# Other places in a hand-planned order of work, the last chunk done for all u at once, and w_o loaded from ScalarE

## The chip, the cores and the metric

The kernel runs on one core of one Trainium2 chip. The metric is the device time of one execution in microseconds (us), the median of several runs. PE is TensorE, DVE is VectorE, ACT is ScalarE, POOL is GpSimd and SP is SyncE, which here issues most DMAs.

## The reference: what is computed

Two strided convolutions with gelu, a joint network, and all gradients. B = 2, T = 16000, D = V = 256, U = 8, three taps; everything in bf16.

```python
h = sum_i einsum("btc,cd->btd", xp[:, i:i+T], w1[i]);  h = gelu(h)[:, ::2]
f = sum_i einsum("btc,cd->btd", hp[:, i:i+T1], w2[i]);  f = gelu(f)[:, ::2]
fe = f @ w_f;  ge = g @ w_g
j = tanh(fe[:, :, None, :] + ge[:, None, :, :])
out = j @ w_o                      # (2, 4000, 8, 256)
# outputs: out and, for a given grad_out, the gradients of x, w1, w2, g, w_f, w_g, w_o
```

The joint part and its gradient are the bulk: 8000 places (b, t) times 8 values of u.

## The kernel before

**Tiling.** The 8000 places lie on one axis and are cut into 17 chunks: one of 256, fifteen of 512 and one of 64 places (`sizes`). A chunk of 512 is nb = 4 blocks of 128; the last is nb = 1, n_ = 64. One chunk holds the border between the two batches (`c.mid`, number CB).

**Stages.** Each chunk passes through three:
- `stage_a`: transposed x arrives in XC by a transposing DMA; conv1 at odd and even places, gelu and its derivative (`conv_gelu`, a Square, a Gelu and a Tanh on ACT and six operations on DVE), conv2 with a gelu, then FE = f w_f. HR is HT transposed by a DMA. From chunk NTR = 2 on, `fe_rows` puts FE row-wise in FER with PE transposes.
- `stage_j`: four pairs of u (`pair(up)`). Per pair: JT = tanh(FE + GE) on ACT, 4 activations; JR, the same row-wise (DVE add of FER and GEB, then ACT tanh; in chunks 0 and 1 PE transposes of JT instead); GWO, the gradient of w_o, as JR times GO in one PSUM bank that is kept over the whole kernel; GOT (GO transposed by a DMA) times WOT, multiplied on DVE with JSQ - 1 (JSQ = JT squared) into NGZ or ZS, whose free-axis sum goes to NGP, and added up in ZS, at last in GN; and out = JT w_o, evicted to OUT and stored. Line 315 is the helper `mm`, so all these matmuls have one line, and tiles tell them apart.
- `stage_de` of the chunk before: the gradient goes back through w_f, w2, w1 (GN, GH, GX) and the weight gradients are added up in ACC1, ACC2, ACCF from row-wise copies HR, GNR, GHR and XR.

**What sets the order of work.** The program records operations with `op(engine, cost, ...)`. Each has a place in a line of work, `F.now` or `at`, counted in places of the axis: chunk k begins at `t0 = c.q0`, and the stages of other chunks stand at fractions of it. `Flow.issue` then plays a model: at each step it emits the operation that can start first, on the engine whose start is earliest, and among those ready, the one of the smallest place. Costs come from `c_pe`, `c_act`, `c_dve`, and a DMA takes its size over a rate, plus `land`. What it emits is the static program order of each engine; nothing is decided at run time. Buffers (`F.cls`: 3 JT, 3 JR, 3 GOT, 4 GO, 3 OUT, 7 PSUM banks) are handed out in this order as well.

**The last chunk.** It runs through the same `pair(up)` with nb = 1 and n_ = 64: PE operands 64 wide, four GO loads, four GOT transposes and four stores of 64 KB each. Behind it `last_w1` does the w1 gradient of the last two chunks together, and the final stores follow.

**The start.** ACT issues the loads of w1 (three), w_f and w_g; SP those of x, w2 and the transposed XC of chunk 1; POOL those of g and w_o. The tiles of w1 and w2 are both called W in the trace. `warm` is an early Gelu on ACT that makes its table load happen early; `make_ge` needs WG, and `turn` transposes WO, WG, WF, W2 and W1 on PE.

Of the kernel before, what the change touches and what calls it, by code (L numbers as in the profile page):

```python
# [10 lines left out]
BF16 = mybir.dt.bfloat16  # L11
# [175 lines left out]


def c_pe(ns):
    return sum(max(n / 2.4 + 2.5, 25.0) for n in ns)  # L190


def c_act(n, psum=False, ptr=False):
# [17 lines left out]
def kernel(  # L211
# [28 lines left out]
    KT = 2  # L240
# [225 lines left out]
    def conv_gelu(g_, jobs, rd, h_buf, pre, ho, gname, gcls, gshape, gsave, news):  # L466
# [36 lines left out]
               r=[qk(mt), ps], w=[sk(mt)])  # L503
        k = GELU_A / 2
        N = KT * W
        late = F.now + CW * (0.8 if g_ == 1 else 0.25)
        go_ = 1 if gsave else 0
        full = lambda T_, o_=0: T_[:, o_:o_ + nb, :, :n_]
        op("ACT", c_act(N), lambda e: nc.scalar.activation(out=full(s, so), in_=full(s, so), func=ACT.Tanh, scale=k),  # L509
# [31 lines left out]
    def stage_a(g_, t0, dt):  # L541
        c = chunks[g_]
        S = st[g_]
        XC = S["XC"]
        nb, n_ = c.nb, c.np
        na = min(nb, 2)
        HT = buf("gh" if c.first else "ht", [P, (2 * NB + 2) if c.first else (3 * NB + 1), KT, P], BF16, "HT")
        oE, oF = nb + 1, 2 * nb + 1
        two = g_ == 1

        def conv1(l0):
            def jobs(mt, h):
# [12 lines left out]
        F.now = t0  # L565
        conv_gelu(g_, conv1(2), [xm[:1] + [W1], xm[:2] + [W1]] if two else [xm + [W1]], HT, "o", 1, "G1o", "g1o", [P, NB + 1, KT, P], "hg1", [HT])
        F.now = t0 + 0.05 * dt
        halo(g_, HT, "o", "HTo", "hho")
        if c.mid:
            pool_zero(lambda: HT[:, 0, :, c.pb:c.pb + 1], [], [(HT, ("o", "h"))])  # L570
        F.now = t0 + 0.12 * dt
# [3 lines left out]
        F.now = t0 + 0.3 * dt  # L575

        def conv2(mt, h):
            lst = []
            seq_ = [(2, 1), (1, oE), (0, 0)]
            for k, (i, o_) in enumerate(seq_):  # L580
                for kt in range(KT):
                    lst.append((lambda ps: ps[:, :c.W],
                                lambda i=i, kt=kt, mt=mt: W2[:, i, kt, mt * P:(mt + 1) * P],
                                lambda o_=o_, kt=kt: HT[:, o_:o_ + nb, kt, :n_],
                                k == 0 and kt == 0, k == 2 and kt == KT - 1))
            return lst, c_pe([c.W] * 6)
        hto = [(HT, ("o", k)) for k in (0, 1, "h", "h0")] + [(HT, ("e", 0)), (HT, ("e", 1))]
# [3 lines left out]
        F.now = t0 + 0.48 * dt  # L591
        FE = S["FE"] = buf("fe", [P, KT, CW], BF16, "FE")
        for mt in range(KT):
            ps = psum()

            def mms(e, mt=mt, ps=ps):
                for kt in range(KT):
                    mm(ps[:, :c.W], WF[:, kt, mt * P:(mt + 1) * P], HT[:, oF:oF + nb, kt, :n_], kt == 0, kt == KT - 1)
            op("PE", c_pe([c.W] * KT), mms, r=ftk + [WF], w=[ps], new=[ps] + ([FE] if mt == 0 else []))
            evac(lambda mt=mt: FE[:, mt, :c.W], lambda ps=ps: ps[:, :c.W], c.W, r=[ps], w=[(FE, mt)])  # L600
        F.now = t0 + 0.55 * dt
        if g_ >= NTR:
            fe_rows(g_)
        F.now = t0 + 0.75 * dt
        tile_rows(g_, "HR", "hr", HT, 3 * nb + 1, shape=[P, 3 * NB + 1, D], land=4500.0)

    def fe_rows(g_):
# [13 lines left out]

    n_gwo = sum(c.nb for c in chunks) * U * KT
    gwo_cnt = [0]
    gwo_ops = []

# [26 lines left out]
    def stage_j(g_, t0, dt):  # L654
# [7 lines left out]
        def pair(up):  # L662
# [4 lines left out]
            for j in range(2):  # L667
                for mt in range(KT):
                    for k_, (lo, hi, b) in enumerate(parts_of(c)):
# [4 lines left out]
                           new=[JT] if j == 0 and mt == 0 and k_ == 0 else [], at=tu - q * (1.0 - (2 * j + mt) / 4))  # L674
            npart = len(parts_of(c))
            for h in range(max(nb // 2, 1)):
                na = min(nb, 2)
                JR = buf("jr", [P, 2, 2, D], BF16, "JR")
                th = tu + q * (h / 2 - 0.5)
                if g_ < NTR:  # L680
                    ps = psum(BF16)

# [19 lines left out]
                def gwo(e, h=h, na=na, JR=JR):  # L702
                    for a in range(na):
                        for j in range(2):
                            for d2 in range(KT):
# [4 lines left out]
                gwo_ops.append(op("PE", c_pe([V] * (4 * na)), gwo, r=[JR, GO], w=[], at=tu + q * (h / 2 + 0.3)))  # L710
            OUT = buf("out", [P, NB, 2, V], BF16, "OUT_SB")
            for step in range(4):
                j, d2 = step // 2, step % 2
# [11 lines left out]
                if d2 == 0:  # L725
                    JSQ = buf("jsq", [P, KT, CW], BF16, "JSQ")

                    def jsq(e, j=j, JSQ=JSQ):
# [2 lines left out]
                        else:  # L731
                            nc.vector.tensor_tensor(out=JSQ[:, :, :W], in0=JT[:, j, :, :W], in1=JT[:, j, :, :W], op=ALU.mult)
                    op(("ACT", "DVE"), (c_act(KT * W), c_dve(KT * W, 0.5)), jsq,
                       r=[(JT, (j, mt, k_)) for mt in range(KT) for k_ in range(npart)], w=[JSQ], new=[JSQ], at=F.now - q / 4)
# [22 lines left out]
                if step < nb:  # L757
# [8 lines left out]
                    op("PE", c_pe([V] * 4), out_mm, r=[JT, WO, (OUT, "b")], w=[ps], new=[ps] + ([OUT] if a == 0 else []))  # L766
# [9 lines left out]

    def pe_rows(g_, name, cls, SRC, lo, nblk, m):
        R = buf(cls, [P, 2 * NB + (cls == "ghr"), D], BF16, name)  # L780
# [8 lines left out]
        op("PE", c_pe([P] * (nblk * KT)), trs, r=[SRC, ident], w=[ps], new=[ps, R])  # L789
        evac(lambda: R[:m, 0:nblk].rearrange("p a d -> p (a d)"), lambda: ps[:m, 0:nblk * D], nblk * D, r=[ps], w=[R], f=0.5)  # L790
        return R

    def grad_rows(g_, name, cls, SRC, nblk, m):
        if chunks[g_].last:
            return pe_rows(g_, name, cls, SRC, 1, nblk, m)
# [42 lines left out]
    def stage_de(g_, t0, dt):  # L838
# [12 lines left out]

        def blx(ps):
            return ps[:, :Wx].rearrange("p (a n) -> p a n", a=nb)
        F.now = t0 + dt * 0.05
        for mt in range(KT):
            ps = psum()

# [60 lines left out]
        for i, o_ in ((1, nb + 1), (0, 0), (2, 1)):  # L918
# [4 lines left out]
        load_xr(g_, t0 - 300.0 if c.last else t0 + dt * 0.3, [got_op[0, UP - 1]] if c.first else ())  # L923
# [139 lines left out]
    def gwg_out():  # L1063
# [8 lines left out]

    BIG = -1e9
    CONVS = 4
    GEBX = 1.2
    F.now = BIG

    warm = buf("gsq", [P, KT, CW], BF16, "g_sq")
    op("DVE", 200.0, lambda e: nc.vector.memset(warm[:, 0, 0:2 * P], 0.0), w=[(warm, 0)], new=[warm])
    op("ACT", 1400.0, lambda e: nc.scalar.activation(out=warm[:, 1, 0:8], in_=warm[:, 0, 0:8], func=ACT.Gelu_apprx_tanh),  # L1080
       r=[(warm, 0)], w=[(warm, 1)])
    wps = psum()

    WARM = 20
# [14 lines left out]
    wload("ACT", WG, 0, lambda: WG[:], lambda: w_g.rearrange("(kt p) n -> p kt n", p=P), BIG, 7000.0)  # L1099
# [5 lines left out]
    wload("POOL", WO, 0, lambda: WO[:], lambda: w_o.rearrange("(kt p) n -> p kt n", p=P), BIG + 2, 9000.0)  # L1105

    def turn(jobs, at, behind=()):

# [48 lines left out]
    for k in range(NG + 1):  # L1157
        c = chunks[min(k, LAST)]
        t0, Wk = float(c.q0 if k < NG else NQ), float(c.W) if k < NG else 300.0
        if k < NG:  # L1160
            if k in (NTR, CB, CB + 1):
                load_geb(c, lambda up, t0=t0, Wk=Wk, k=k: t0 + Wk * (up / UP - (GEBX if k == NTR else 0.5)))
            for up in range(UP):
                load_go(k, up, t0 + Wk * (up // 2 * 2 / UP - 0.6), [got_op[0, up - 2]] if k == 0 and up > 1 else ())
                load_got(k, up, t0 + Wk * (up / UP - 0.6))
        if 0 < k < LAST:
            load_xc(k + 1, t0 - Wk * 0.3)
        if k < NG:
            stage_j(k, t0, Wk)
        if k + 1 < NG:  # L1170
            stage_a(k + 1, t0, Wk)
        if k >= 1:
# [46 lines left out]
```

## Time and profile before

| | |
|---|---|
| Median of 3 runs | 782.3 us (781.51 to 782.38) |
| Profiled execution | 781.06 us |
| Its span, first to last instruction | 779.0 us |
| TensorE clock granted | 0.999 |
| Matmuls | 5641 |
| HBM | 52.99 MB read, 50.35 MB written |
| DMA, all queues | 183.82 MB, mean 236 GB/s |
| SP's queue | 181.64 MB, 391226 packets |

Times in the profile are of one execution. An engine's busy time is the union of its instructions; a matmul's bar includes the time until its result is out, so that successive bars overlap, and the distance between two starts tells what one costs. In the timeline a row is a run of like instructions: start, length, engine, line, operation, output and inputs, shape, count, and in brackets the idle time before it with what ended it.

### The profile page before, as it was taken

The page shows a single profiled execution, that of the slowest core. Times are in us where ns is not written, and L with a number is a line of the kernel's source. Part 1 is how long each engine was busy: PE and PEld are TensorE (multiplying, and loading weights), DVE is VectorE, ACT ScalarE, POOL GpSimd, SP SyncE. Part 2 cuts the span into 40 slices and gives each one's busy share as a digit, 9 for nine tenths or more (in the row PEclk, how much of TensorE's full clock was granted, in tenths as well). Part 3 has the DMA queues.
Part 4 walks back from the last instruction along what each step waited for, and adds up shares of the span by engine and source line. Part 5 has one row for each costly group of instructions (what it writes and reads, how often), then busy time and mean ns, then how long its engine had stood idle before and what let it go on. Part 6 is the DMA issues. An engine that isn't in the chain of part 4 may idle for free.

```text
span 779.0 us, 15414 instructions
## 1 busy us (share of the span) xinstructions
PE 767.7 (99%) x5641; PEld 533.0 (68%) x5641; DVE 718.2 (92%) x1511; ACT 710.5 (91%) x1145; POOL 84.0 (11%) x223
## 2 busy tenths in 40 slices
PE   8999999999999999999999999999999999999997
PEld 6765767576676766767577675766767667677765
DVE  4989999998999999999999999989999899999874
ACT  5989999999999999999999999899999999999752
POOL 2001010101102010020110202001020010201000
PEclk9999999999999999999999999999999999999999
DMA  9999999999999999999999999999999999989783
GB/s 182 228 250 230 230 232 265 250 228 273 205 252 241 240 293 223 280 236 238 257 252 283 204 249 252 236 283 212 272 238 223 254 223 291 191 225 244 187 177 109
DMA packets 393624, 183.82 MB, mean 236 GB/s; under 512 B 318145, under 2 KB 386668, under 8 KB 391628
## 3 DMA queue, kind: packets, MB, share of 16 engines
q1 hardware_dynamic: 391226, 181.64, 102.5%
q10 hardware_dynamic: 2178, 1.05, 0.5%
q8 instruction: 44, 0.72, 0.4%
q0 software_dynamic: 144, 0.15, 0.2%
q14 instruction: 32, 0.26, 0.1%
HBM read 52.99 MB, written 50.35 MB: 133 GB/s over the span
## 4 chain that ended last, share of the span: by engine, by line
PE 89%; ACT 6%; DVE 3%; DMA 2%; issue 1%; ACTq 0%
PE ps L315 74%; PE GWO L315 14%; ACT JT L670 2%; DMA WG<-in_w_g_dram 1%; PE psb L616 1%; ACT JSQ L730 1%; ACT HT L499 1%; ACT g_sq L497 1%; DMA W<-in_w_dram 0%; DVE NGZ L739 0%; ACT JR L699 0%; ACT OUT_SB L324 0%; DVE g_s L501 0%; DVE ZS L754 0%; ACT g_s L509 0%
## 5 line engine op out<-in xcount | busy, mean ns | idle before, releaser
L670 ACT ACTIVATE JT<-FE,GE 128x512 bf16<-128x512 bf16 (+4 forms) x288 | 178.9, 683 | 0.0
L739 DVE SCALAR_TENSOR_TENSOR NGZ<-JSQ,ps 128x512 f32<-128x512 bf16 (+3 forms) x252 | 150.8, 607 | 2.1 <-PE ps L315 1.9
L315 PE MATMUL ps<-WO,JT 128*128 128x256 bf16 (+1 forms) x1008 | 150.5, 273 | 0.3 <-DVE NGZ L739 0.2
L315 PE MATMUL ps<-GOT,WOT 128*128 128x512 bf16 (+2 forms) x544 | 149.9, 362 | 0.3 <-DVE g_s L501 0.3
L730 ACT ACTIVATE JSQ<-JT 128x1024 bf16<-128x1024 bf16 (+2 forms) x129 | 131.0, 1015 | 11.1 <-DVE NGZ L739 8.3
L315 PEld LDWEIGHTS <-JT 128*128 128x128 bf16 (+1 forms) x1008 | 98.3, 98 | 58.3 <-issue 0.4
L324 ACT CAST OUT_SB<-ps 128x512 bf16<-128x512 f32 (+1 forms) x205 | 121.7, 605 | 14.8 <-PE ps L315 14.3
L699 ACT ACTIVATE JR<-JR 128x1024 bf16<-128x1024 bf16 (+1 forms) x116 | 123.5, 1066 | 9.6 <-DVE JR L694 9.6
L315 PE MATMUL GWO<-GO_R,JR 128*128 128x256 bf16 (+1 forms) x1008 | 130.8, 273 | 0.6 <-DVE JR L329 0.6
L754 DVE TENSOR_TENSOR ZS<-ZS,NGZ 128x1024 f32<-128x1024 f32 (+2 forms) x102 | 115.3, 1130 | 0.7
L315 PEld LDWEIGHTS <-JR 128*128 128x128 bf16 (+1 forms) x1008 | 98.2, 98 | 15.8 <-DVE JR L329 0.9
L315 PEld LDWEIGHTS <-W 128*128 128x128 bf16 x636 | 60.0, 98 | 59.8 <-issue 0.7
L315 PE MATMUL ps<-W1T,GH 128*128 128x256 bf16 (+2 forms) x506 | 94.6, 325 | 1.3 <-ACT FE L324 1.2
L315 PE MATMUL ps<-XC,W 128*128 128x512 bf16 (+2 forms) x432 | 86.5, 351 | 0.1
L315 PE MATMUL ps<-GHR,XR 128*128 128x256 bf16 (+1 forms) x736 | 83.3, 273 | 0.0
L315 PEld LDWEIGHTS <-XR 128*128 128x128 bf16 (+1 forms) x756 | 73.7, 98 | 8.6
L694 DVE TENSOR_TENSOR JR<-FER,GEB 128x1024 bf16<-128x1024 bf16 (+1 forms) x116 | 78.0, 673 | 0.0
L315 PEld LDWEIGHTS <-WOT 128*128 128x128 bf16 x544 | 51.0, 98 | 29.6 <-issue 1.9
L819 DVE TENSOR_TENSOR ACC<-ACC,ps 128x512 f32<-128x512 f32 x87 | 57.4, 679 | 14.4 <-PE ps L315 14.3
L315 PEld LDWEIGHTS <-GH 128*128 128x128 bf16 (+1 forms) x506 | 49.4, 98 | 26.3 <-issue 1.9
L326 ACT ACTIVATE GX_SB<-ps 128x512 bf16<-128x512 f32 (+1 forms) x89 | 52.0, 608 | 13.8 <-PE ps L315 13.5
L497 ACT ACTIVATE g_sq<-ps 128x512 bf16<-128x512 f32 (+2 forms) x102 | 57.6, 565 | 2.8 <-PE ps L315 2.8
(131 smaller groups left out, 984.2 us busy)
## 6 DMA issues: line engine op xcount, KB each, us to landing
GO_R<-in_grad_out_dram SPq DMA_DIRECT2D x60, 512.0 KB, 5.2
out_dram<-OUT_SB SPq DMA_DIRECT2D x60, 512.0 KB, 5.5
XR<-in_x_dram SPq DMA_DIRECT2D x15, 1088.0 KB, 8.6
out_dram<-GX_SB SPq DMA_DIRECT2D x30, 512.0 KB, 3.3
GOT<-GO_R SPq DMA_TRANSPOSE x68, 5.3
GO_R<-in_grad_out_dram SPq DMA_DIRECT2D x4, 256.0 KB, 4.1
out_dram<-OUT_SB SPq DMA_DIRECT2D x4, 256.0 KB, 2.6
out_dram<-STAGE SPq DMA_DIRECT2D x6, 128.0 KB, 1.8
```

The costliest lines, as they stand in the source:

```text
L315: nc.tensor.matmul(ps_ap, lhsT=lhsT, rhs=rhs, start=start, stop=stop)
L324: nc.scalar.copy(out=dst(), in_=src())
L326: nc.scalar.activation(out=dst(), in_=src(), func=ACT.Copy, scale=scale)
L497: op("ACT", c_act(W, True), lambda e, mt=mt, ps=ps: nc.scalar.activation(out=sq[:, 0:nb, mt, :n_], in_=blk(ps, c), func=ACT.Square, scale= ...
L499: op("ACT", c_act(W, True), lambda e, mt=mt, ps=ps: nc.scalar.activation(out=h_buf[:, ho:ho + nb, mt, :n_], in_=blk(ps, c), func=ACT.Gelu_ ...
L670: op("ACT", c_act((hi - lo) * nb, ptr=True), lambda e, j=j, mt=mt, lo=lo, hi=hi, b=b: nc.scalar.activation(out=cut(JT[:, j, mt, :W], lo, h ...
L694: op("DVE", c_dve(na * 2 * D, 0.5), lambda e, h=h, na=na, JR=JR: nc.vector.tensor_tensor(out=JR[:n_, 0:na], in0=S["FER"][:n_, 2 * h:2 * h ...
L699: op("ACT", c_act(na * 2 * D), lambda e, na=na, JR=JR: nc.scalar.activation(out=JR[:n_, 0:na], in_=JR[:n_, 0:na], func=ACT.Tanh), r=[JR], ...
L730: nc.scalar.activation(out=JSQ[:, :, :W], in_=JT[:, j, :, :W], func=ACT.Square)
L739: nc.vector.scalar_tensor_tensor(out=cut(Z[:, d2, :W], lo, hi), in0=cut(JSQ[:, d2, :W], lo, hi), scalar=1.0, in1=cut(ps[:, :W], lo, hi), o ...
L754: nc.vector.tensor_tensor(out=o_, in0=i0, in1=i1, op=ALU.add)
L819: op("DVE", c_dve(512), lambda e: nc.vector.tensor_tensor(out=acc_ap().rearrange("p k d -> p (k d)"), in0=acc_ap().rearrange("p k d -> p ( ...
```

## The change

1. **Places.** Many `at` and `F.now` fractions are other numbers: conv2, FE, HR, the row-wise JR, the GWO matmuls, the squares, GOT, XC, XR. In the changed kernel GWO and out matmuls of the last two pairs of the last chunk but one are given places 130 and 100 later (`DEFER`). The model's price of a matmul has a floor of 45 ns instead of 25, which only matmuls under 102 columns feel.
2. **The last chunk** gets functions of its own, `load_last` and `stage_j_last`. They put all 8 u times 64 places on one axis of 512: one GO tile of 128 rows (two u halves of 64 places, two DMAs), one transposing DMA for GOT, 16 JT activations of 64 columns, 8 PE transposes for JR (no FER, no row-wise tanh), GOT products of 512 columns, two multiplies, two reductions and three halving adds on DVE, 8 GWO and 8 out matmuls, two stores. Its work has place t0 + 100, its activations t0 - 64, its loads t0 - 154.
3. **w_o** is loaded from ACT's queue behind w_g, instead of POOL's; the warm Gelu has a place behind ACT's loads.

The diff, cut:

```diff
-    return sum(max(n / 2.4 + 2.5, 25.0) for n in ns)
+    return sum(max(n / 2.4 + 2.5, 45.0) for n in ns)
...
-        late = F.now + CW * (0.8 if g_ == 1 else 0.25)
+        late = F.now + CW * ({2: 0.17, 1: 0.61}.get(g_, 0.25))
...
# stage_a: halo 0.05 -> 0.08, conv1 even 0.12 -> 0.10, conv2 0.3 -> 0.20, FE 0.48 -> 0.38, HR 0.75 -> 0.84
-        if g_ >= NTR:
+        if NTR <= g_ < LAST:
             fe_rows(g_)
...
# pair(up)
-                th = tu + q * (h / 2 - 0.5)
+                th = tu + q * (h / 2 - 0.56)
...
-                gwo_ops.append(op("PE", ..., gwo, ..., at=tu + q * (h / 2 + 0.3)))
+                gwo_ops.append(op("PE", ..., gwo, ..., at=tu + q * (h / 2 + 0.49) + DEFER.get((g_, up), 0.0)))
...
# squares: at F.now - q / 4 -> F.now - q * 0.16
...
+                    op("PE", c_pe([V] * 4), out_mm, ..., at=F.now + DEFER.get((g_, up), 0.0))
...
+    def load_last(at):
+        c, S = chunks[LAST], st[LAST]
+        n_ = c.np
+        GO = S["GO4"] = buf("go", [P, 2, UP, V], BF16, "GO_R")
+        src = gof[c.q0:c.q0 + n_].rearrange("n (a h) v -> n a h v", h=2)
+        for h in range(2):
+            dma("SP", lambda h=h: GO[h * n_:(h + 1) * n_, 0], lambda h=h: src[:, :, h, :], ...)
+        GOT = S["GOT4"] = buf("got", [P, 2, UP, KT, P], BF16, "GOT")
+        dma("SP", lambda: GOT[:, 0]..., lambda: GO[:, 0]..., ..., transpose=True, at=at)
+
+    def stage_j_last(t0):
+        F.now = t0 + LATE[0]
+        JT = buf("jt", [P, 2, KT, CW], BF16, "JT")
+        for u in range(U):
+            for mt in range(KT):
+                op("ACT", ..., out=JT[:, 0, mt, u * n_:(u + 1) * n_], in_=S["FE"][:, mt, :n_], Tanh, ..., at=t0 - 64.0)
+        JR = buf("jr", [P, UP, D], BF16, "JR")
+        # 8 transposes of JT into one PSUM bank, one eviction to JR
+        # JSQ = JT * JT on DVE
+        for d2 in range(KT):
+            # ps = WOT x GOT, 2 matmuls of 512 columns; NGZ[d2] = (JSQ - 1) * ps on DVE
+        F.now = t0 + LATE[2]
+        # per d2: tensor_reduce NGZ over n into NGP; then NGZ halves added, 256, 128, 64 wide, the last into GN
+        F.now = t0 + LATE[1]
+        # GWO: 8 matmuls JR x GO;  out: 2 x 4 matmuls JT x WO, 2 evictions, 2 stores from SP
...
# grad_rows, last chunk: buffer class "hr" in place of "ghr"; XR 0.3 -> 0.29; the first matmul of stage_de 0.05 -> 0.04
+    LEAD = 0.3
+    LATE = (100.0, 100.0, 100.0)
+    DEFER = {(LAST - 1, 3): 100.0, (LAST - 1, 2): 130.0}
+    EARLY = 0.0
...
-       r=[(warm, 0)], w=[(warm, 1)])
+       r=[(warm, 0)], w=[(warm, 1)], at=BIG + 5.0)
...
-    wload("ACT", WG, 0, lambda: WG[:], ..., BIG, 7000.0)
+    wload("ACT", WG, 0, lambda: WG[:], ..., BIG, 6500.0)
+    wload("ACT", WO, 0, lambda: WO[:], ..., BIG, 7000.0)
...
-    wload("POOL", WO, 0, lambda: WO[:], ..., BIG + 2, 9000.0)
...
-                load_got(k, up, t0 + Wk * (up / UP - 0.6))
+                load_got(k, up, t0 + Wk * (up / UP - 0.71))
...
-            load_xc(k + 1, t0 - Wk * 0.3)
+            load_xc(k + 1, t0 - Wk * 0.21)
```

More of the change, by code (lines that the diff above doesn't have):

```diff
@@ L566, in stage_a @@
         conv_gelu(g_, conv1(2), [xm[:1] + [W1], xm[:2] + [W1]] if two else [xm + [W1]], HT, "o", 1, "G1o", "g1o", [P, NB + 1, KT, P], "hg1", [HT])
-        F.now = t0 + 0.05 * dt
+        F.now = t0 + 0.08 * dt
         halo(g_, HT, "o", "HTo", "hho")
@@ L574, in stage_a @@
         pad_tail(g_, HT, "e", (oE, oE + nb))
-        F.now = t0 + 0.3 * dt
+        F.now = t0 + 0.20 * dt
         def conv2(mt, h):
@@ L590, in stage_a @@
         pad_tail(g_, HT, "f", (oF, oF + nb))
-        F.now = t0 + 0.48 * dt
+        F.now = t0 + 0.38 * dt
         FE = S["FE"] = buf("fe", [P, KT, CW], BF16, "FE")
@@ L620, in fe_rows @@
              r=[ps], w=[FER], f=0.5)
-    n_gwo = sum(c.nb for c in chunks) * U * KT
+    n_gwo = sum(c.nb * U for c in chunks[:LAST]) * KT + UP * KT
     gwo_cnt = [0]
@@ L673, in pair @@
                            r=[(S["FE"], mt), (GE, b)], w=[(JT, (j, mt, k_))],
-                           new=[JT] if j == 0 and mt == 0 and k_ == 0 else [], at=tu - q * (1.0 - (2 * j + mt) / 4))
+                           new=[JT] if j == 0 and mt == 0 and k_ == 0 else [], at=tu - q * (1.00 - (2 * j + mt) / 4))
             npart = len(parts_of(c))
@@ L733, in pair @@
                     op(("ACT", "DVE"), (c_act(KT * W), c_dve(KT * W, 0.5)), jsq,
-                       r=[(JT, (j, mt, k_)) for mt in range(KT) for k_ in range(npart)], w=[JSQ], new=[JSQ], at=F.now - q / 4)
+                       r=[(JT, (j, mt, k_)) for mt in range(KT) for k_ in range(npart)], w=[JSQ], new=[JSQ], at=F.now - q * 0.16)
                 Z = ZS if first else NGZ
@@ L765, in out_mm @@
                                    kt == 0, kt == KT - 1)
-                    op("PE", c_pe([V] * 4), out_mm, r=[JT, WO, (OUT, "b")], w=[ps], new=[ps] + ([OUT] if a == 0 else []))
+                    op("PE", c_pe([V] * 4), out_mm, r=[JT, WO, (OUT, "b")], w=[ps], new=[ps] + ([OUT] if a == 0 else []),
+                       at=F.now + DEFER.get((g_, up), 0.0))
                     evac(lambda a=a: OUT[:n_, a].rearrange("p u v -> p (u v)"), lambda ps=ps: ps[:n_, :], 512,
@@ L775, in stage_j @@
             pair(up)
+    def load_last(at):
[4 more added lines that the diff above has]
+        for h in range(2):
+            dma("SP", lambda h=h: GO[h * n_:(h + 1) * n_, 0], lambda h=h: src[:, :, h, :], r=[], w=[(GO, h)],
+                bytes_=n_ * 2048, new=[GO] if h == 0 else [], land=4500.0, load=True, at=at)
+        GOT = S["GOT4"] = buf("got", [P, 2, UP, KT, P], BF16, "GOT")
+        dma("SP", lambda: GOT[:, 0].rearrange("p a k n -> p (a k) n"), lambda: GO[:, 0].rearrange("p a v -> p (a v)"),
+            r=[GO], w=[GOT], bytes_=UP * KT * P * P * 2, new=[GOT], land=4500.0, transpose=True, at=at)
@@ L779, in pe_rows @@
     def pe_rows(g_, name, cls, SRC, lo, nblk, m):
-        R = buf(cls, [P, 2 * NB + (cls == "ghr"), D], BF16, name)
+        R = buf(cls, [P, 3 * NB + 1 if cls == "hr" else 2 * NB, D], BF16, name)
         st[g_][name] = R
@@ L788, in trs @@
                                         in_=SRC[:, lo + a, kt, :m], identity=ident[:])
-        op("PE", c_pe([P] * (nblk * KT)), trs, r=[SRC, ident], w=[ps], new=[ps, R])
+        op("PE", c_pe([P] * (nblk * KT)), trs, r=[SRC, ident], w=[ps], new=[ps, R], at=F.now - EARLY)
         evac(lambda: R[:m, 0:nblk].rearrange("p a d -> p (a d)"), lambda: ps[:m, 0:nblk * D], nblk * D, r=[ps], w=[R], f=0.5)
@@ L853, in blx @@
             return ps[:, :Wx].rearrange("p (a n) -> p a n", a=nb)
-        F.now = t0 + dt * 0.05
+        F.now = t0 + dt * 0.04
         for mt in range(KT):
@@ L922, in stage_de @@
             tick()
-        load_xr(g_, t0 - 300.0 if c.last else t0 + dt * 0.3, [got_op[0, UP - 1]] if c.first else ())
+        load_xr(g_, t0 - 300.0 if c.last else t0 + dt * 0.29, [got_op[0, UP - 1]] if c.first else ())
         ghk = [(GH, ("o", k)) for k in (0, 1)] + [(GH, ("e", k)) for k in (0, 1, "h", "h0", "z")] + ([(GH, "m")] if c.mid else [])
@@ L1098 @@
     wload("ACT", WF, 0, lambda: WF[:], lambda: w_f.rearrange("(kt p) n -> p kt n", p=P), BIG, 6500.0)
-    wload("ACT", WG, 0, lambda: WG[:], lambda: w_g.rearrange("(kt p) n -> p kt n", p=P), BIG, 7000.0)
+    wload("ACT", WG, 0, lambda: WG[:], lambda: w_g.rearrange("(kt p) n -> p kt n", p=P), BIG, 6500.0)
+    wload("ACT", WO, 0, lambda: WO[:], lambda: w_o.rearrange("(kt p) n -> p kt n", p=P), BIG, 7000.0)
     for b in range(B):
@@ L1162 @@
                 load_geb(c, lambda up, t0=t0, Wk=Wk, k=k: t0 + Wk * (up / UP - (GEBX if k == NTR else 0.5)))
-            for up in range(UP):
-                load_go(k, up, t0 + Wk * (up // 2 * 2 / UP - 0.6), [got_op[0, up - 2]] if k == 0 and up > 1 else ())
-                load_got(k, up, t0 + Wk * (up / UP - 0.6))
+            if k == LAST:
+                load_last(t0 - CW * LEAD)
+            for up in range(UP if k < LAST else 0):
+                load_go(k, up, t0 + Wk * (up // 2 * 2 / UP - 0.60), [got_op[0, up - 2]] if k == 0 and up > 1 else ())
+                load_got(k, up, t0 + Wk * (up / UP - 0.71))
         if 0 < k < LAST:
-            load_xc(k + 1, t0 - Wk * 0.3)
+            load_xc(k + 1, t0 - Wk * 0.21)
         if k < NG:
-            stage_j(k, t0, Wk)
+            stage_j(k, t0, Wk) if k < LAST else stage_j_last(t0)
         if k + 1 < NG:
```

71 lines of the change are left out of this document (66 added, 5 removed).

## The prediction

> **What bounds it now.** I read the page first, then stretches of the span, then the chain of work that ended last, and last the timeline of the final 45 us, because the change has one part at the start, one at the end and one everywhere between.
>
> ```profile
> PE 767.7 (99%) x5641; PEld 533.0 (68%) x5641; DVE 718.2 (92%) x1511; ACT 710.5 (91%) x1145; POOL 84.0 (11%) x223
> ...
> PE 89%; ACT 6%; DVE 3%; DMA 2%; issue 1%; ACTq 0%
> ```
>
> PE is the bound, but a busy bar is longer than a matmul's slot (273 ns for 256 columns), so I measured slots as differences of starts. In the timeline 48 matmuls of 256 columns begin at 734.15 and the next group at 739.39: 0.109 us each. Two of 512 columns take 739.39 to 739.82: 0.216 each. A 128-column transpose takes half of 0.109, by starts 0.056. A 512-column chunk in the steady part has 104 matmuls of 512, 224 of 256 and 8 transposes: 104 x 0.2158 + 224 x 0.1092 + 8 x 0.056 = 47.35 us. The chain shows the same group of 22 matmuls at 303.15 and 350.54, and at 541.24 and 588.63: a period of 47.39. So the steady part holds no idle time that an order of work could win back.
>
> ```profile
> 0.00:20.00 20.00, 17.29 (x158) 13.63 (x159) 9.06 (x33) 11.59 (x28) 5.76 (x20) 1.00 0.93 183
> 20.00:70.00 50.00, 46.67 (x373) 32.93 (x372) 46.64 (x116) 45.79 (x82) 6.19 (x18) 1.00 1.12 232
> ...
> 410.00:740.00 330.00, 330.00 (x2410) 229.70 (x2408) 312.75 (x629) 310.00 (x489) 34.74 (x88) 1.00 1.03 239
> 740.00:775.00 35.00, 34.57 (x290) 23.96 (x288) 24.40 (x83) 16.68 (x40) 2.04 (x10) 1.00 0.61 146
> 775.00:779.00 4.00, 0.00 (x0) 0.00 (x0) 0.04 (x1) 0.26 (x1) 0.00 (x0) 0.89 0.44 117
> ```
>
> Columns after the stretch: its length, then PE, weight load, DVE, ACT, POOL. Summing over all matmuls the time between two starts less the slot above, PE loses 5.7 us in 0 to 20, 6.2 in 20 to 70, 0.7 in 370 to 410, 2.8 in 740 to 775 and about 1 elsewhere: 16.4. Nothing else can be saved except work itself, and the 4.8 us after the last matmul starts.
>
> **The end: work removed.** This is the surest term. The last chunk has 64 places, and its four pairs run small matmuls.
>
> ```profile
> 744.61 0.22 PE L315 MATMUL ps<-GOT,WOT 128*128 128x64 bf16 x2
> 744.76 0.62 PE L315 MATMUL ps<-WO,JT 128*64 128x256 bf16 x4
> 745.32 0.23 PE L315 MATMUL ps<-GOT,WOT 128*128 128x64 bf16 x2
> 745.48 0.61 PE L315 MATMUL GWO<-GO_R,JR 64*128 64x256 bf16 x4
> 746.02 0.29 PE L315 MATMUL ps<-GOT,WOT 128*128 128x64 bf16 x4
> ```
>
> Starts are in the first column. Four matmuls with a 64-wide operand take 0.56 and 0.54 us, where four full ones take 0.437 (740.69 to 741.13): each change of array shape costs about 0.1. Over the chunk by starts: 32 GOT matmuls 1.76, 16 WO 2.23, 16 GWO 2.16, two transposes of FE rows 0.23; sum 6.38. After the change: 8 transposes 0.45, 4 GOT of 512 columns 0.86, 8 GWO 0.87, 8 WO 0.87; sum 3.05. **Saved: 3.3 us**, and PE stands nearly back to back until 774.5, so it should all reach the end.
>
> One page speaks of these slots: the Trainium skill, "TensorE: Matmul & The Clock Gate", section "Back-to-back issue gap", gives N/2.4 + 2.5 ns with a floor near 25 ns for up to 64 columns, and nothing for a change of shape. By it the old work would be about 4.5 us, the saving an estimated 1.5 and the whole sum -3.2 instead of -5.0. The trace has 57 ns for two uninterrupted 64-column matmuls (760.75 to 760.80), which agrees, and the 0.1 us changes beside it, which do not; the measured sum decides.
>
> What is late next is the chain of the last chunk: GOT products 0.43, the first multiply 0.68 and the second 0.68, two reductions over 512 columns (not in the trace: between 0.30, the reduction over 144, and 1.21, the 1024-wide add; I take 0.65, the 512-wide add into an accumulator being 0.69), three halving adds (512, 256, 128 columns: 0.67, 0.4, 0.29), so about 4.5 us to GN. From GN (763.95) to the end the run before took 15.0, of which three groups of 16 GHR matmuls (1.84 each) were queued ahead of it: about 9.5 bare. That makes 14 us of chain. Beside it lie the late matmuls: 48 of the chunk before (5.2), the rest of the last chunk (about 8): 13.2. The two deferred pairs of the chunk before (16 WO and 16 GWO matmuls each, 7.0 us in all, formerly at 730 to 744) fill the earlier waits for transposes. The cover is about as long as the chain, so I keep 3.3 with bounds of 0 and 4.5 (3.3 and half of the 2.8 lost). Deferring holds JR: four halves wait and there are three buffers, so one DVE add (0.68) and ACT tanh (1.06) come late; DVE is busy 24.4 of the last 35 us. Two 512 KB stores follow the deferred products: 5.5 us to landing from perhaps 763 is 769, before the end. Fewer small DVE and ACT operations (about 1.5 us and 4 us) gain nothing themselves. The last chunk's loads become three DMAs for eight, with SP idle after 764.
>
> **The start: w_o on ACT.** The chain's first pieces are:
>
> ```profile
> 0.74 3.43 DMA W<-in_w_dram
> 4.19 9.90 DMA WG<-in_w_g_dram
> ```
>
> WG is issued only at 4.19, when the first W piece has landed and freed its semaphore, lands at 14.09, and PE waits 1.7 us for it; ACT's chain follows from there. With WO off POOL and on ACT's queue the gelu table load (1.24 to 2.52) comes after six issues of 0.37 to 0.49 us each; its cover is ACT's first copy at 6.40. If WG no longer waits, it goes out near 2.9: a gain of at most 1.3, and PE's wait caps it at 1.7. But WO, issued at 2.72 and landed 9.2 us later, is now behind WG and lands later; its transpose at 16.47 is before conv2's followers, and the planner, told that it lands sooner, may place it sooner: a new wait between 0 and 1.7. I take **-0.7**, bounds -1.7 and +1.0. POOL's freed 0.76 us has no waiter.
>
> **The moved places.** 512 columns are 47.4 us. conv2 and FE go 4.7 us earlier in the order, HR's transpose and the next XC 4.3 later, GOT 5.2 earlier, GWO's matmuls 2.3 later, JR 0.7 earlier, the squares 1.1 later. Later transfers have cover: HR is issued at 540.15 and read at 582.1; XC at 572.40 and read at 610.9. GOT has the least, 5.5 us from landing to use at 319.09, and gains. GWO later gives JR more time and keeps GO and JR longer; GO's next load has that same 5 us. In the steady part I cost all this at nothing; PE's full queue hides it, and the price if that cover goes is the second rival. The lost 6.2 us between 20 and 70 come with DVE at 46.6 and ACT at 45.8 of 50, so most stays; from the shift of chunks 1 and 2 I take -0.8 (bounds -3 and +2), and -0.2 of the 0.7 in the middle chunk.
>
> **Sum**: -3.3 - 0.7 - 0.8 - 0.2 = -5.0 on a profiled execution of 781.06 (span 779.0 and 2.06 around it), 776.1. The median 782.3 lies 1.2 above that execution, within 0.2%, which is about what a measurement of this kernel can tell from no change. On the median: 777.3; the case's own range is 774.5 to 779.5.
>
> **Rivals.**
> 1. *The stall only moves* (0.15). WO takes WG's place: PE waits at WO's transpose and the start gains nothing: -4.3, **778.0**. For: one queue, 128 KB more on it; against: three queues already shared DMA engines at a share of 0.93. The Trainium skill, "DMA: Bandwidth & Descriptors", section "Issuing engines are not separate DMA queues", says that DMAs from all engines interleave on the same 16 engines, which gives this case; WO's 9.2 us and WG's 9.9 from two different queues agree.
> 2. *Steady stalls, slower* (0.15). conv2 and FE earlier put a gelu's DVE and ACT work ahead of the operations that free PSUM; DVE has 17 us of slack in 330, ACT 20, about 2.5 per chunk. If one 512-column eviction (0.69) per chunk comes late, 14 chunks lose 9.7: **787.0**. It decides from 5.0/14 = 0.36 us per chunk. Against: no PE wait in 410 to 740 now.
> 3. *The end becomes the chain* (0.13). The last chunk stands at place 8036, after the chunk before is done; each microsecond by which chain exceeds cover is idle PE. If it eats all 3.3: **780.6**.
> 4. *The ramp gives more* (0.15). Half of the 6.2 (-3.1) and the whole wait for WG (-1.7): -8.3, **774.0**.
> That the moved places change no order at all in the steady part would leave the forecast as it is.
>
> **How the numbers follow.** The forecast has 0.42. Faster by over 0.2% (below 780.7): forecast, rivals 1 and 4 and a part of 3: 0.77. Within 0.2%: the rest of 3 and mild forms of 2: 0.09. Slower: 0.14. The range reaches from rival 4's case with more of the end (772.5) over rival 3 to a mild rival 2 (783.0), and leaves out the bulk of rival 2.
>
> **What would show it.** After: the period stays 47.39 (else rival 2, seen as PE waits on DVE or ACT); GOT matmuls of 64 columns are gone; the last matmul starts near 769; between 745 and there PE loses under 3 us (else rival 3); WG is issued before 4.19 and PE's wait is for WO or for nothing (rival 1); the loss in 20 to 70 is 5 to 6 us (else 4). A period over 47.7 would prove me wrong at once.

## The result and the profile after

The changed kernel takes 771.4 us (median of 4 runs, 771.3 to 771.85), the kernel before 782.3 (781.51 to 782.71): a ratio of 0.9864, 95% interval 0.9851 to 0.9877. It is 10.9 us faster and lies 1.1 us below the low end of the forecast range. The profiled execution after took 771.4 us, with a span of 769.6.

The page after, engines and the chain that ended last by engine:

```profile
PE 761.3 (99%) x5603; PEld 531.2 (69%) x5603; DVE 720.8 (94%) x1486; ACT 699.9 (91%) x1121; POOL 96.3 (13%) x222
...
PE 88%; DVE 0%; DVEq 0%; ACT 0%; issue 0%
```

PE is the bound as before, and the pieces that ACT (6%) and the DMA of WG (1%) had in the chain are gone. Stretches of the span after, columns as in the prediction:

```profile
0.00:20.00 20.00, 18.58 (x181) 14.96 (x182) 11.41 (x39) 13.90 (x34) 4.98 (x19) 1.00 0.85 202
20.00:70.00 50.00, 47.66 (x388) 34.49 (x386) 47.08 (x116) 46.99 (x83) 5.06 (x18) 1.00 1.12 245
...
410.00:740.00 330.00, 329.99 (x2407) 229.36 (x2405) 316.80 (x639) 304.35 (x483) 45.14 (x88) 1.00 1.01 240
740.00:765.00 25.00, 25.00 (x207) 18.07 (x204) 15.85 (x33) 8.96 (x16) 2.12 (x11) 1.00 0.59 155
```

181 matmuls begin in the first 20 us, where 158 did, and the last one begins at 764.9, where it was 774.2. In the steady part nothing moved: a piece of the chain of PE begins at 210.83 and its like at 258.17, a period of 47.34 (47.39 before).

Below, *loss* is what the prediction defined: time between two matmul starts less the slot. Summed by stretch, before to after: 0 to 20 us 5.74 to 3.70; 20 to 70 6.20 to 3.29; 70 to 370 0.29 to 0.36; 370 to 420 (the middle chunk) 0.69 to 0; 420 to 720 0.41 to 0.41; behind 720 3.04 to 0.75, with 1.37 us less matmul work; behind the last matmul 0.13 less. Together 9.37, which is the difference of the spans (778.96 and 769.59). Of the rest of the 10.9, 1.3 us is that the profiled execution before lay that much below its median, and 0.3 lies outside the spans; the section on the start shows why that kernel's executions differ.

### The profile page after: what moved, and what is told of

It reads as the page before. It is cut to its first block, busy times and chain, and to the rows that moved or that the text cites. A ratio compares the mean times of both kernels' runs of the same rounds, so it can differ in the third digit from the quotient of the medians.

```text
span 769.6 us, 15273 instructions
## 1 busy us (share of the span) xinstructions
PE 761.3 (99%) x5603; PEld 531.2 (69%) x5603; DVE 720.8 (94%) x1486; ACT 699.9 (91%) x1121; POOL 96.3 (13%) x222
## 4 chain that ended last, share of the span: by engine, by line
PE 88%; DVE 0%; DVEq 0%; ACT 0%; issue 0%
PE ps L315 74%; PE GWO L315 13%; PE psb L616 1%; DVE NGZ L739 0%; DVE GN L754 0%; DVEq L1311 0%; DVE JR L694 0%; PE psb L878 0%; PE psb L814 0%; ACT GX_SB L326 0%; PE psb L1150 0%; DVE GX_SB L331 0%
## 5 line engine op out<-in xcount | busy, mean ns | idle before, releaser
L670 ACT ACTIVATE JT<-FE,GE 128x512 bf16<-128x512 bf16 (+3 forms) x272 | 175.7, 692 | 0.0
L315 PE MATMUL ps<-WO,JT 128*128 128x256 bf16 x1000 | 148.1, 273 | 0.1
L315 PE MATMUL ps<-GOT,WOT 128*128 128x512 bf16 (+1 forms) x516 | 147.3, 372 | 0.0
L739 DVE SCALAR_TENSOR_TENSOR NGZ<-JSQ,ps 128x512 f32<-128x512 bf16 (+2 forms) x238 | 147.3, 630 | 0.0
L730 ACT ACTIVATE JSQ<-JT 128x1024 bf16<-128x1024 bf16 (+1 forms) x124 | 129.8, 1050 | 9.6 <-DVE NGZ L739 6.8
L315 PEld LDWEIGHTS <-JT 128*128 128x128 bf16 x1000 | 97.7, 98 | 59.2 <-DVE W1T L329 0.3
L699 ACT ACTIVATE JR<-JR 128x1024 bf16<-128x1024 bf16 x112 | 119.4, 1066 | 17.4 <-DVE JR L694 17.2
L315 PE MATMUL GWO<-GO_R,JR 128*128 128x256 bf16 x1000 | 129.6, 273 | 0.8 <-DVE JR L329 0.8
L324 ACT CAST OUT_SB<-ps 128x512 bf16<-128x512 f32 x192 | 112.6, 593 | 8.5 <-PE ps L315 7.0
L754 DVE TENSOR_TENSOR ZS<-ZS,NGZ 128x1024 f32<-128x1024 f32 (+1 forms) x96 | 113.4, 1182 | 0.4
```

What stands on the lines that cost most here:

```text
L315: nc.tensor.matmul(ps_ap, lhsT=lhsT, rhs=rhs, start=start, stop=stop)
L324: nc.scalar.copy(out=dst(), in_=src())
L670: op("ACT", c_act((hi - lo) * nb, ptr=True), lambda e, j=j, mt=mt, lo=lo, hi=hi, b=b: nc.scalar.activation(out=cut(JT[:, j, mt, :W], lo, h ...
L699: op("ACT", c_act(na * 2 * D), lambda e, na=na, JR=JR: nc.scalar.activation(out=JR[:n_, 0:na], in_=JR[:n_, 0:na], func=ACT.Tanh), r=[JR], ...
L730: nc.scalar.activation(out=JSQ[:, :, :W], in_=JT[:, j, :, :W], func=ACT.Square)
L739: nc.vector.scalar_tensor_tensor(out=cut(Z[:, d2, :W], lo, hi), in0=cut(JSQ[:, d2, :W], lo, hi), scalar=1.0, in1=cut(ps[:, :W], lo, hi), o ...
```

## Experiments: which part gave how much

Three parts were put on the kernel before one by one, and two were taken from the changed kernel. Times vary by a few tenths of a per cent, so the loss by stretch carries the finer readings. "Conv" is the time from the first conv1 matmul to the first conv2 matmul of chunk 0.

| kernel | conv1 starts | conv | loss 20-70 | 370-420 | behind 720 | ratio to before, interval |
|---|---|---|---|---|---|---|
| before | 8.38 | 6.36 | 6.20 | 0.69 | 3.04 | 1 |
| after | 7.55 | 4.78 | 3.29 | 0.00 | 0.75 | 0.9864 (0.9851-0.9877) |
| e1_start | 8.52 | 4.78 | 5.89 | 0.69 | 3.04 | 0.9961 (0.9946-0.9976) |
| e2_last | 7.48 | 8.44 | 4.87 | 0.69 | 0.75 | 0.9952 (0.9937-0.9967) |
| e3_places | 8.24 | 5.98 | 3.48 | 0.00 | 2.72 | 0.9956 (0.9937-0.9975) |
| e4_no_start | 7.87 | 5.83 | 3.66 | 0.00 | 0.75 | 0.9907 (0.9875-0.9939) |
| e5_no_places | 7.49 | 4.79 | 5.87 | 0.69 | 0.75 | 0.9917 (0.9891-0.9944) |
| s1_wo_act | 8.37 | 4.78 | 5.89 | 0.69 | 3.04 | 0.9966 (0.9954-0.9977) |
| s2_warm_late | 8.02 | 4.79 | 5.88 | 0.69 | 3.04 | 0.9963 (0.9948-0.9977) |
| s3_xc_waits | 7.26 | 4.79 | 4.21 | 0.69 | 3.04 | 0.9954 (0.9938-0.9971) |
| r1_late_old | 7.79 | 4.78 | 3.64 | 0.00 | 0.75 | 0.9879 (0.9850-0.9908) |
| r2_conv2_old | 7.39 | 4.79 | 3.63 | 0.23 | 0.75 | 0.9875 (0.9841-0.9909) |
| r3_pairs_old | 7.24 | 4.79 | 4.90 | 0.20 | 0.75 | 0.9893 (0.9875-0.9911) |
| r4_dma_old | 7.40 | 4.78 | 5.76 | 0.00 | 0.75 | 0.9896 (0.9881-0.9911) |
| q_got_old | 8.40 | 4.79 | 5.59 | 0.00 | 0.75 | 0.9900 (0.9874-0.9927) |
| q_xc_old | 7.23 | 4.79 | 3.29 | 0.00 | 0.75 | 0.9866 (0.9839-0.9892) |
| q_gwo_old | 7.77 | 4.79 | 4.75 | 0.00 | 0.75 | 0.9882 (0.9859-0.9906) |
| e7_no_defer | 7.17 | 4.79 | 3.31 | 0.00 | 1.42 | 0.9869 (0.9841-0.9897) |

**e1_start**, the start alone:

```diff
+ at=BIG + 5.0                       # the warm Gelu
- wload("POOL", WO, ...)
+ wload("ACT", WO, ..., BIG, 7000.0) # and WG's landing 7000 -> 6500
```

> The kernel before with only the start of the change (w_o on ACT's queue, the warm Gelu behind the loads, the two landing times in the model). Theory A, the three parts add up: PE's loss in 0 to 20 us falls from 5.7 to about 3.7 us as in the changed kernel, WG's wait is gone, the XC transposes end their issue near 10.3 instead of 13.8, and the time falls by 2.0 to 2.8 us (ratio 0.9964 to 0.9974). Theory B, the ramp takes it back: the same start, but the loss in 20 to 70 us grows by as much, and the time changes by less than 0.8 us.

Conv is 4.78 as in the changed kernel, the loss in 20 to 70 stays at 5.89: theory A, 779.2 against 781.8 (the ratio, 0.9961, is just below its range). The loss in 0 to 20 us is 4.7 and not the 3.7 of theory A, because conv1 began 1.0 us later than in the changed kernel's profile; the last section comes back to this.

**e2_last**: the last chunk's functions, `DEFER` and the 45 ns floor alone.

> The kernel before with only the last chunk done for all u at once (with the deferred pairs and the 45 ns floor). Theory A: PE work falls by 3.3 us, the stretch from the period's end to the last matmul shortens by 3.0 to 4.0 us, the time falls by as much (ratio 0.995 to 0.996), and nothing ahead of 700 us changes by over 0.5 us. Theory B, the end becomes a chain: PE loses over 3 us behind 745 us and the time falls by less than 1 us.

778.3. The loss behind 720 falls to 0.75, the work by 1.37, as in the changed kernel: 3.66 together. Of the ramp's loss one pause of 1.35 only slid past 70 us. PE's wait for the first weights is longer in this execution (3.0 us for WF, then WG), which the expectation had not allowed for: conv is 8.44. The clock fell behind it, as the section on the start shows.

**e3_places**: all moved places alone.

> The kernel before with only the moved places. Theory A: the loss in 20 to 70 us falls from 6.2 to about 3.3 and that in 370 to 410 from 0.7 to 0; the time falls by 2.8 to 4.0 us (ratio 0.995 to 0.9965). Theory B, the ramp's gain in the changed kernel came from its earlier start and not from the places: the loss in 20 to 70 stays over 5 us and the time falls by less than 1.5 us.

778.3. The loss in 20 to 70 is 3.48 and the middle chunk's 0: theory A; the start did not make the ramp's gain.

**e4_no_start** and **e5_no_places**: the changed kernel without the start, and without the moved places.

> The changed kernel with the start as before (w_o on POOL, warm Gelu in front). If the parts add up: PE waits 1.5 to 3.5 us for WG, the loss in 20 to 70 and behind 720 us stays as in the changed kernel (3.3 and 0.75 us), and the time is 2.0 to 3.5 us above 771.4. If the ramp could absorb the start, the loss in 20 to 70 would fall by over 1 us and the time would rise by less than 1.2 us.

> The changed kernel with all old places. If the parts add up: the loss in 20 to 70 us is 5.5 to 6.5, that in the middle chunk 0.7, the end as in the changed kernel, and the time is 3.0 to 4.5 us above 771.4. If the places mattered only together with the old start or the old end, the time is within 1.2 us of 771.4.

774.7 and 775.3. Each brings back its own stretch and no other; the stall that e4 brings back is 1.0 us in this execution, less than the 1.5 expected. In e5 the pauses of the ramp are those of the kernel before one by one, 2.4 us earlier (the pause of 1.35 us at 66.70 for 69.12). The three ratios of the parts alone multiply to 0.9870; the whole has 0.9864. By medians the parts give 2.6, 3.5 and 3.5 us, 9.5 of the 10.9. **The parts add up**, within these intervals.

## Experiments: the start

Every kernel with the old start has a conv of 5.8 to 8.4 us, every other 4.78 or 4.79: the stall on the first weights is 1.0 to 3.7 us long and differs from one execution to the next. A long stall costs more than its length. In e2's trace the granted clock is 0.5 from 15.09 to 18.51 us, behind the wait of 3.0 us, which by an estimate (half of 3.4) is 1.7 us of lost matmul time; in the profile of the kernel before, with a stall of 1.58, it stays at 1.00 from 14 to 18 us. Over the 38 runs of the kernel before, the 12 with a mean granted clock of 0.997 or less have a median of 783.2 us, the 18 with 0.999 or more 781.1, and the 8 in between 782.4. That longer stalls made these runs longer is likely but not shown, since only profiled runs have the clock in time.

Three single edits of the kernel before ask what makes the stall.

**s1_wo_act**: w_o on ACT, nothing else. **s2_warm_late**: `at=BIG + 5.0` for the warm Gelu, nothing else. **s3_xc_waits**:

```diff
- load_xc(1, BIG, 60.0)
+ load_xc(1, BIG, 60.0, after=w1_ops[:1])    # the transposing DMA waits for the first w1 piece
```

> The kernel before with w_o loaded from ACT's queue behind w_g and nothing else (the warm Gelu in front, so that ACT's second load stands behind it in the model's order). If POOL's queue beside XC's transposes was the cost, WG lands before 13 us and PE's wait for it is under 0.5 us. If the cost is that XC's transposes go out ahead of WG, then WG is still issued behind a landing near 4.2 us, XC's first issue stays near 2.2 us, PE waits 1.5 to 3.6 us for WG or WO, and the time stays within 1 us of the kernel before.

> The kernel before with only the warm Gelu placed behind ACT's loads; w_o stays on POOL. If the order of the issues is what matters: WG becomes one of the first eight transfers and goes out near 2.8 us, XC's first transpose then waits for a landing until 3.7 to 4.3 us, PE does not wait for WG, and the time falls as with the whole start part, by 2.0 to 2.8 us. If moving w_o off POOL matters, PE still waits over 1 us for WG and the time stays within 1 us.

> The kernel before in which the transposing load of chunk 1's XC may go out only after the first w1 piece has landed; w_o stays on POOL, the warm Gelu in front, WG's issue still waits for the same landing near 4.2 us. Theory C, the start's gain is the XC transposes no longer running beside the weight loads: XC's issue ends near 10 to 11 us, WG lands before 12.5 us, PE's wait for it falls from 1.7 to under 0.3, and the time falls by 1 to 2.5 us. Theory D, the gain is WG's own earlier issue and the short queue in front of it: WG still lands near 14 us, PE waits over 1.2 us for it and the time stays within 0.8 us.

All three remove the whole stall: s1 as its first case had it, s2 as its first, and s3 as theory C. s2 and s3 fell by 3.1 and 3.4 us, more than was expected; s3 also loses less in the ramp (4.21). But they share neither WG's own issue (4.10 in s1, 2.81 in s2, 4.32 in s3) nor XC's first issue (2.2, 4.2 and 5.3), so no single one of these is the whole cause. What they share shows in the stretch from 8 to 10 us; the last columns of the first line are the DMA engines' busy share and GB/s. Below it stand the DMA queues of the same 2 us: packets, MB, and the share of the 16 engines' time (q0 is POOL's, q1 SP's, q10 ACT's). The kernel before:

```profile
8.00:10.00 2.00, 1.92 (x18) 1.51 (x16) 0.42 (x1) 0.86 (x3) 0.44 (x2) 1.00 1.21 114
...
q0 software_dynamic: 32, 0.09, 61.0%
q1 hardware_dynamic: 492, 0.13, 57.4%
```

The same stretch of s1_wo_act:

```profile
8.00:10.00 2.00, 1.92 (x18) 1.51 (x16) 0.42 (x1) 0.86 (x3) 0.44 (x2) 1.00 1.28 245
...
q1 hardware_dynamic: 1605, 0.41, 111.9%
q10 hardware_dynamic: 154, 0.08, 16.3%
```

The DMA engines are as busy, but in the kernel before they move half the bytes. In the same stretch e4, with the old start, has 104 GB/s, s2 218 and s3 288. The old start alone has both w_o on POOL's queue and XC's transposes issued ahead of WG; take away either one, and WG is there in time.

The packets in the traces show where the engines' time went. From POOL's queue w_o moves as 32 packets of 4096 bytes, from ACT's as 256 packets of 512. In the four profiles with the old start the 32 packets pass beside XC's transposes and take 0.44 to 0.75 us each on average. XC's packets of 256 bytes there take 0.025 to 0.032 us on average in the first 20 us. In s2 and s3 the same 32 packets pass before most or all of XC's, and take 0.21 and 0.19 us each; XC's take 0.021 and 0.024. So the slow loads go with w_o's large packets in flight beside the transposes. That these are the cause is not shown by an experiment of its own: s1 changes the packets, but also issues w_o at 4.52 instead of 2.72 us and behind WG, and s3 also let two loads of GO go ahead of XC. In the timeline of the changed kernel (start, length, engine, line, operation) ACT has these rows:

```profile
2.81 0.49 ACTq L341 DMA_DIRECT2D WG<-in_w_g_dram  x1
4.05 0.39 ACTq L341 DMA_DIRECT2D WO<-in_w_o_dram  x1
4.47 1.28 ACT L1175 ACT_TABLE_LOAD   x1 [4.47 <-DMA W<-in_w_dram]
5.77 0.21 ACT L1175 ACTIVATE g_sq<-g_sq 128x8 bf16<-128x8 bf16 x1
5.88 0.57 ACT L324 COPY XC<-psb 128x512 bf16<-128x512 bf16 x1
```

and SP's queue, in the same view:

```profile
3.69 6.57 SPq L339 DMA_TRANSPOSE XC<-in_x_dram  x2
10.31 1.34 SPq L341 DMA_DIRECT2D GO_R<-in_grad_out_dram  x2
```

WG goes out at 2.81 (4.19 before), w_o waits for a landing in its stead, the table load stands behind it and ends just before the first copy; and XC's two transposes, though begun 1.5 us later, are through the queue at 10.3 instead of 13.8.

## Experiments: the ramp

Of the moved places, which carry the 2.9 us between 20 and 70? Each kernel is the changed one with one group at its old place.

```diff
# r1_late_old:   {2: 0.17, 1: 0.61}.get(g_, 0.25)  ->  0.8 if g_ == 1 else 0.25
# r2_conv2_old:  conv2 0.20 -> 0.3, FE 0.38 -> 0.48
# r3_pairs_old:  JR 0.56 -> 0.5, GWO 0.49 -> 0.3, squares 0.16 -> 0.25
# r4_dma_old:    HR 0.84 -> 0.75, GOT 0.71 -> 0.6, XC 0.21 -> 0.3, XR 0.29 -> 0.3
# q_got_old:     GOT 0.71 -> 0.6      q_xc_old: XC 0.21 -> 0.3      q_gwo_old: GWO 0.49 -> 0.3
```

> The changed kernel with the old places of the gelu derivative's last operations in chunks 1 and 2 (0.8 and 0.25 of a chunk behind instead of 0.61 and 0.17). Theory E, the ramp's gain comes from these two: the loss in 20 to 70 us returns from 3.3 to over 5 us and the time rises by 1.5 to 3 us against the changed kernel's 771.4. Theory F, it comes from conv2 and FE standing 4.7 us earlier: the loss stays under 4 us and the time within 0.8 us.

> The changed kernel with conv2 and FE at their old places (0.30 and 0.48 of a chunk instead of 0.20 and 0.38). Theory F: FE of the next chunk comes late again, waits of PE, DVE or ACT on FE stand near 60 to 70 us, the loss in 20 to 70 us is over 5 us and the time rises by 1.5 to 3 us against 771.4. Theory E: the loss stays under 4 us and the time within 0.8 us; the middle chunk's 0.7 us may come back in either case.

772.3 and 772.0, losses 3.64 and 3.63: both theories fall as the main cause.

> The changed kernel with the places inside a pair as before (row-wise JR 0.5 instead of 0.56 of a pair ahead, GWO's matmuls 0.3 instead of 0.49 behind, the squares 0.25 instead of 0.16 ahead). Theory G, these free ACT and PE for what PE waits on in the ramp: the two or three pauses near 57 to 69 us (2.8 us before) come back, the loss in 20 to 70 us is over 5 us, the time 1.5 to 3 us above 771.4. Rival H, no single group of places carries it, each order of the ramp loses 3.3 to 4.5 us unless all are as they were: the loss is under 4.5 us and the time within 1.2 us.

> The changed kernel with the places of the transfers as before (HR 0.75, GOT 0.6, XC 0.3, XR 0.3). Theory I, the ramp was waiting for transfers: the loss in 20 to 70 us rises by over 1.5 us and waits of PE on DMA appear. What the trace of before says, with no wait of PE on a DMA between 20 and 740 us: the loss stays within 0.7 us of 3.3, no wait on DMA, and the time within 0.8 us of 771.4.

772.9 with a loss of 4.90, which lies between theory G and rival H, and 773.5 with 5.76. r4 refutes what I expected of it: the transfers' places matter most. But its other theory fails too, since PE waits on no DMA there.

> The changed kernel with GOT's transposes alone at their old place (0.6 instead of 0.71 of a chunk ahead); on PE 2688 lines of the program order differ from the changed kernel's. If the 2.5 us that came back with all old places of transfers hang on GOT: the loss in 20 to 70 us is over 5 us, PE's waits there are on DVE and ACT and none on a DMA, and the time is 1.5 to 2.5 us above 771.4. If they hang on XC: the loss stays under 4 us.

> The changed kernel with XC's load alone at its old place (0.3 instead of 0.21); 149 lines of PE's order differ. If the 2.5 us hang on XC: the loss in 20 to 70 us is over 5 us and the time 1.5 to 2.5 us above 771.4. If they hang on GOT: loss under 4 us, time within 0.8 us.

> The changed kernel with GWO's matmuls alone at their old place (0.3 instead of 0.49 of a pair behind), which changes the most lines of any single place (12757 on PE). If the 1.6 us that came back with all old places inside a pair hang on it: the loss in 20 to 70 us is 4.5 to 5.5 us, with waits of GWO on JR of 1.1 us or more, and the steady part stays at a loss under 1 us in 70 to 720. If they hang on JR's place: the loss stays near 3.3 us.

**GOT's place alone** brings back 2.3 us of loss in the ramp (5.59), XC's none, and GWO's 1.5 (4.75), which is all of r3. The two don't add: with all old places the ramp loses 5.87 (e5). The times are 774.4, 771.8 and 773.3; q_got's is more than was expected and above that of r4, which has the same edit among others; in its profile conv1 began 1.0 us later than in r4's and 70 to 370 us lost 1.6 more, so the ramp's loss carries the reading. Yet PE in q_got waits on no DMA between 20 and 75 us, nor does DVE or ACT. PE's waits there, the longest first, with total, number and longest:

```profile
PEld L315 <- DVE JR L329: 2.0, 2, 1.1
PEld L315 <- issue: 1.8, 6, 0.4
PE GWO L315 <- DVE JR L329: 1.6, 2, 0.8
PEld L616 <- issue: 0.9, 1, 0.9
PEld L688 <- ACT JT L670: 0.7, 1, 0.7
PE psb L616 <- ACT OUT_SB L324: 0.6, 1, 0.6
```

PE waits for what DVE and ACT evict or make. An earlier place of a transfer lets the planner believe the transposed gradient ready sooner, and it then emits the computing in another order. By the names of the tiles, the orders in the traces of q_got and of the changed kernel differ from 37 us on, in 424 lines of a diff for PE's matmuls, 150 for DVE and 120 for ACT (the 2688 of the expectation counts the program's lines); a shift of GOT by 0.01 changes not one line of the program. So the place acted through the order, not through a wait for the transfer. A pause that the new order removed looks so in the timeline of the kernel before, on PE:

```profile
68.79 0.60 PE L315 MATMUL ps<-WO,JT 128*128 128x256 bf16 x4
70.58 1.14 PE L315 MATMUL ps<-W1T,GH 128*128 128x512 bf16 x6 [1.19 <-ACT FE L324]
```

and on ACT at that time:

```profile
68.06 1.05 ACT L509 ACTIVATE G<-G 128x1024 bf16<-128x1024 bf16 x1
69.01 1.05 ACT L730 ACTIVATE JSQ<-JT 128x1024 bf16<-128x1024 bf16 x1
69.95 1.06 ACT L324 CAST FE<-ps 128x512 bf16<-128x512 f32 x2
```

The FE products were ready before 69, but their eviction stood behind a tanh and a square on ACT, and PE had to wait until the first of the two evictions had emptied its PSUM bank. In the timeline of the changed kernel PE runs on behind the same FE products (HT, WF):

```profile
65.02 1.03 PE L315 MATMUL ps<-HT,WF 128*128 128x512 bf16 x4
65.89 0.60 PE L315 MATMUL ps<-WO,JT 128*128 128x256 bf16 x4
66.32 0.81 PE L315 MATMUL ps<-W1T,GH 128*128 128x512 bf16 x4
66.97 1.91 PE L315 MATMUL ps<-GNR,HR 128*128 128x256 bf16 x16
```

In 20 to 70 us ACT and DVE are busy 45.8 and 46.6 us in the kernel before and 47.0 and 47.1 in the changed one, so a better order was to be had without less work. In q_got PE also waits 0.6 us on GOT itself and 0.8 on GHR behind 75 us, which it does not in the changed kernel's profile. That an earlier GOT gives slack there too is not shown: it is one execution, and e7 below has such waits in the changed kernel's own order.

## Experiments: the end

**e7_no_defer**: `DEFER = {}`.

> The changed kernel without the deferral of the two last pairs of the chunk before the last. If the deferred 7 us of matmuls are the cover under which the last chunk's chain runs: PE loses 2 to 4 us more behind 720 us (0.75 now) and the time rises by 2 to 4 us. If the last chunk's chain has cover without them: the loss behind 720 us stays under 1.5 us and the time within 0.8 us of 771.4.

772.5, loss behind 720 1.42 against 0.75: two waits on DVE's GH products (1.1 us on the weight load) that the deferred matmuls had covered. The loss is as the second case had it, but the time, 1.1 us above the changed kernel's, fits neither case. In the profile PE also waits twice, at 245 and 292 us, on the DMA of GNR (1.2 us of loss); its order there is the changed kernel's, which differs only from 716 us on. So the deferral is worth 0.7 us by the trace, and the last chunk's chain had its cover without it. DVE's timeline of the changed kernel shows that chain:

```profile
743.40 1.28 DVE L829 SCALAR_TENSOR_TENSOR NGZ<-JSQ,ps 128x512 f32<-128x512 bf16 x2
744.59 1.27 DVE L834 TENSOR_REDUCE NGP<-NGZ 128x8 f32<-128x512 f32 x2
...
747.35 0.29 DVE L841 TENSOR_TENSOR GN<-NGZ 128x128 bf16<-128x128 f32 x1
```

The GOT products begin at 742.59 and GN is there at 747.64: 5.05 us (4.5 forecast). PE's first matmuls on this GN begin only at 753.54, and at 747.64 it has 17 us of matmuls left, more than the 9.5 of bare chain.

## Why the prediction was wrong

- **Wrong as a whole**: the forecast was -5.0, the measured change -10.9, and the range stopped at 772.5. The likely direction, the bound on PE, the free steady part and the end were right; rival 4, a larger gain, was the right case at 774.0, and too small.
- **The step that failed most: the ramp term of -0.8.** Measured: -2.9 by the trace, and -0.7 instead of -0.2 in the middle chunk. The argument was that DVE and ACT are busy over 90% there, so most of the loss stays. e3 and e5 show that the same work in another order loses 3.3 to 3.7 (after, e3, e4) instead of 5.9 to 6.2 (before, e1, e5), at nearly the same busy time. The step that failed is the one from a high busy share to pauses that must stay: in the pause shown above, what counted was which of ACT's operations came first, not ACT's total.
- **The start term of -0.7.** The loss in 0 to 20 us fell by 2.04. The stall of 1.58 (6.36 less 4.78) is gone whole, 0.4 us of other waits came in behind it, and 0.8 is the earlier beginning of conv1, which varies between executions (8.52 in e1, with the new start) and is not the change's. So the trace gives -1.2; the median of e1 gives -2.6, with the interval 1.9 to 4.2 (0.9946 to 0.9976 of 781.8). I capped the gain at the 1.7 us of one profiled execution, though the stall varies from 1.0 to 3.7 and a long one can take clock with it, and I set against it a wait on w_o that did not come: rival 1 is refuted by e1 and s1, in which no wait on a DMA of WO or WG is left. Rival 1 cited the Trainium skill ("DMA: Bandwidth & Descriptors", section "Issuing engines are not separate DMA queues"), which also says that issuing from several engines saves the time of issuing alone. s1 (0.9966, 0.9954 to 0.9977) gains more than that by the choice of queue, but it also changes when w_o is issued and in what packets, so it does not test that rule by itself.
- **The median.** I added 1.2 us to both sides alike. The changed kernel has no varying stall, and its profiled execution is at its median; that step cost 1.3.
- **The end, -3.3, was right**: 3.66 by the trace in e2 and in the changed kernel. Most of the 2.29 of it that stands as less loss is the changes of array shape, which the forecast counted as work (6.38 by starts, about 4.6 by slots). The 2.8 of loss that its bound of 4.5 drew on held them a second time. Rival 3 (the chain) is refuted by e7. The two reductions, not in the trace before, took 1.27 together, with 1.30 taken.
- **Rival 2 (steady stalls)** is refuted: the period is 47.34.
- Of the transfers I wrote that later ones have cover and GOT "gains". No trace speaks against either, and both missed the point: their places changed the order of computing.

## What to carry to other kernels

In a planned order, a place is read by the planner before it is read by the chip: moving a transfer that nobody waits for reordered PE, DVE and ACT here, so the order itself must be compared, not only the slack. Pauses of a bound engine in a ramp are worth counting one by one, with what stands ahead of the releaser on its engine; a neighbour's high busy share doesn't say that they must stay. A wait on a DMA seen in one execution is a sample: look at how the runs' times spread before capping its price.

## What was not expected of the hardware

- In 8 to 10 us the DMA engines moved 114 GB/s at a busy share of 1.21 in the kernel before, and 245 at 1.28 in s1, which has the same loads with one of them issued from another queue and later. The 4096-byte packets of that load, from POOL's queue, took 0.75 us each on average beside DMA transposes, and 0.19 to 0.21 largely ahead of them (s2, s3).
- The first 20 matmuls of every kernel are the same, but how long 256 columns take 0.21 us before they take 0.109 varies between executions: the first conv1 matmul stands between 7.17 and 8.52 us over 18 profiles, and 0.8 us of the profiled difference is of this kind. The traces' clock records show the step: the full clock is granted from 3.85 us on at the earliest (e7) and from 7.00 at the latest (e1), though PE's first matmul begins at 1.06 us in all 18.
